# Splitting a fused retention and MLP kernel into up and down phases, with paired attention blocks, quadrant matmuls, DMA transposes and a half-chunk lead-in

## Chip, cores, metric

One core of one Trainium2 chip. The metric is the device time of one execution in microseconds. The profile gives a span, from the first to the last instruction, which is some 2 us shorter. In the profiles PE is the tensor engine (matmuls), DVE the vector engine, ACT the scalar engine, POOL or gpsimd the general one, and SP the one that only issues transfers. In the kernel before, all loads go out on gpsimd's DMA queue and the stores on SP's; the change puts the DMA transposes, and v of units 0 to 3, on SP's too.

## Reference

```python
# q, k, v: (8, 8, 576, 64); w_in: (512, 2048); w_out: (2048, 512)
scores = (q @ k.T) / 8
gamma  = 1 - 2.0 ** (-5 - arange(8))                 # one decay per head
ret    = scores * where(rel >= 0, gamma ** rel, 0)   # rel = query position - key position
x      = (ret @ v) as (4608, 512)                    # tokens x (heads * 64)
h      = x @ w_in
out    = (h * sigmoid(1.702 * h)) @ w_out            # float32
```

The attention is linear, so it runs in units of 128 tokens: scores inside a unit, plus an inter term, q times a running state of k and v from the units before. There are 36 units. Four units make a chunk of 512 tokens, and there are 9 chunks. The product with w_in is called the up projection, that with w_out the down projection, and `h * sigmoid(1.702 * h)` the Gelu; one "up" is the four matmuls that make 128 columns of `h` for a chunk.

## The kernel before

Each iteration `t` of one loop does one unit of attention on PE, a quarter of the up projection of one chunk and a quarter of the down projection of another, alternating.

```python
def transposes(u):                        # k and q: 8 transposes of 128x128 on PE
    for t, (src, nm) in enumerate(((kn[sl], "kn"), (qn[sl], "qn"))):
        for hp in range(HP):
            op("pe", lambda e, ...: e.matmul(psT[:, (1 - t) * HP + hp, :],
                src[:, 2 * hp : 2 * hp + 2, :], ident.ap(), is_transpose=True), ...)
    op("dve", lambda e: e.tensor_copy(qkT[u % 3].ap(), psT.ap()), ...)

def inter(u):                             # 4 matmuls of 128x128, zeros off the block diagonal
    ...
def scores(u):   ...                      # 8 matmuls, 64 rows each
def values(u):   ...                      # 8 matmuls, 64 columns each

load_qk(0); setup(); load_v(0)            # all loads on the gpsimd queue, in this order
for u in range(1, 4): load(u)
for i in range(4):
    load_win(i)
    load(4 + i)
for t in range(-2, NU + LAG):             # NU = 36, LAG = 12
    if t + 2 < NU: scale_v(t + 2)
    if 0 <= t < NU: state(t)
    if t + 2 < NU: transposes(t + 2)
    if 0 <= t < NU:
        state_out(t); inter(t)
        if t < 4: load_wout(t)
        load(t + NLD)                     # NLD = 8 load buffers
    ...                                   # scores of t + 1, values of t
    for s in range(4):
        if 0 <= ch < NCH: up(ch, 4 * hq + s, nh); ...
        if 0 <= co < NCH: down(co, r, s, bank)
    if 0 <= co < NCH: down_out(co, r, bank)
```

## Time and profile before

| | us |
|---|---|
| Median time (3 runs) | 338.76 |
| Span in the profile | 336.7 |
| First up matmul | 33.8 |
| 1152 projection matmuls of 512 columns, 0.863 us per four | 248.6 |
| One unit of attention on PE | 1.66 |

The page of the kernel before, in part: the busy tenths in 40 slices of 8.4 us, and who holds the chain that ended last.

```profile
PE   1676999999999999999999999999999999999995
DMA  9999999996666907667666907001000001011122
GB/s 83 190 196 218 215 210 214 221 202 88 98 88 86 153 31 98 91 95 93 95 93 94 158 31 95 31 33 31 33 31 33 31 34 62 31 33 62 62 94 64
...
PE 89%; POOL 6%; DMA 3%; ACT 0%; issue 0%; POOLq 0%
```

PE is full from the fifth slice on, and the chain is 89% PE: what comes off PE's stream comes off the time. For the first 75 us the loads keep the DMA engines over 90% busy, at about 210 GB/s.

The timeline of PE for one unit of attention before the change (start, duration, line, output and inputs). Matmuls are pipelined, so read the starts, not the durations.

```profile
141.54 0.39 PE L305 MATMUL psK<-vp,kn 128*128 128x128 bf16 x4
141.76 0.39 PE L293 MATMUL psT<-ident,kn 128*128 128x128 bf16 x4
141.98 0.39 PE L293 MATMUL psT<-ident,qn 128*128 128x128 bf16 x4
142.21 0.39 PE L326 MATMUL psO<-qkT,kv_1 128*128 128x128 bf16 x4
142.53 0.40 PE L342 MATMUL psS<-qkT 64*128 64x128 bf16 x8
142.85 0.24 PE L359 MATMUL psO<-pm_0,vp 128*64 128x128 bf16 x1
...
143.20 1.04 PE L374 MATMUL psH<-xT,w_in_sb 128*128 128x512 bf16 x4
```

The unit takes 143.20 - 141.54 = 1.66 us, of which the transposes are 0.44. Inter starts at 142.21 and four matmuls need 0.22, but scores start 0.32 later: 0.10 us is lost where the array shape changes from 128*128 to 64*128. The same happens at the next two changes of shape.

### The profile page before, as it was taken

The page shows a single profiled execution, that of the slowest core. Times are in us where ns is not written, and L with a number is a line of the kernel's source. Part 1 is how long each engine was busy: PE and PEld are TensorE (multiplying, and loading weights), DVE is VectorE, ACT ScalarE, POOL GpSimd, SP SyncE. Part 2 cuts the span into 40 slices and gives each one's busy share as a digit, 9 for nine tenths or more (in the row PEclk, how much of TensorE's full clock was granted, in tenths as well). Part 3 has the DMA queues.
Part 4 walks back from the last instruction along what each step waited for, and adds up shares of the span by engine and source line. Part 5 has one row for each costly group of instructions (what it writes and reads, how often), then busy time and mean ns, then how long its engine had stood idle before and what let it go on. Part 6 is the DMA issues. An engine that isn't in the chain of part 4 may idle for free.

```text
span 336.7 us, 5221 instructions
## 1 busy us (share of the span) xinstructions
PE 316.9 (94%) x2272; PEld 162.5 (48%) x2272; DVE 132.6 (39%) x229; ACT 115.4 (34%) x198; POOL 108.5 (32%) x135
## 2 busy tenths in 40 slices
PE   1676999999999999999999999999999999999995
PEld 0444455555555555555555555555555544443442
DVE  2687766864444434444444434444443200000000
ACT  5400345443333333333333333333333344442211
POOL 8999976842322514222322604000000000000000
PEclk9999999999999999999999999999999999999999
DMA  9999999996666907667666907001000001011122
GB/s 83 190 196 218 215 210 214 221 202 88 98 88 86 153 31 98 91 95 93 95 93 94 158 31 95 31 33 31 33 31 33 31 34 62 31 33 62 62 94 64
DMA packets 87447, 32.85 MB, mean 98 GB/s; under 512 B 76416, under 2 KB 80512, under 8 KB 87424
## 3 DMA queue, kind: packets, MB, share of 16 engines
q0 software_dynamic: 82176, 23.08, 60.3%
q1 hardware_dynamic: 5248, 9.44, 8.1%
q8 instruction: 18, 0.29, 0.4%
q14 instruction: 5, 0.04, 0.0%
HBM read 36.70 MB, written 9.44 MB: 137 GB/s over the span
## 4 chain that ended last, share of the span: by engine, by line
PE 89%; POOL 6%; DMA 3%; ACT 0%; issue 0%; POOLq 0%
PE psH L374 38%; PE psY L392 31%; PE psS L392 4%; PE psT L293 4%; PE psO L359 3%; DMA qn<-in_q_dram 3%; PE psS L342 3%; PE psO L392 2%; POOL kn L200 2%; PE psK L305 2%; POOL vn L214 2%; POOL qn L200 2%; PE psO L326 1%; POOL w_in_sb L223 1%; ACT osb L401 0%; PE psO L332 0%
## 5 line engine op out<-in xcount | busy, mean ns | idle before, releaser
L379 ACT ACTIVATE gT<-psH 128x512 bf16<-128x512 f32 x144 | 86.0, 597 | 182.9 <-PE psH L374 182.9
L374 PE MATMUL psH<-xT,w_in_sb 128*128 128x512 bf16 x576 | 145.1, 381 | 0.0
L392 PE MATMUL psY<-w_out_sb,gT 128*128 128x512 bf16 x480 | 122.2, 379 | 0.7 <-ACT osb L401 0.7
L374 PEld LDWEIGHTS psH<-xT,w_in_sb 128*128 128x128 bf16 x576 | 52.6, 98 | 65.4 <-ACT gT L379 5.1
L392 PEld LDWEIGHTS psY<-w_out_sb,gT 128*128 128x128 bf16 x480 | 46.5, 98 | 57.9 <-ACT osb L401 2.4
L296 DVE COPY qkT<-psT 128x1024 bf16<-128x1024 bf16 x36 | 24.8, 690 | 108.0 <-PE psT L293 107.9
L200 POOL DMA_DIRECT2D kn<-in_k_dram x40 | 36.8, 928 | 94.8 <-PE psK L305 80.3
L214 POOL DMA_DIRECT2D vn<-in_v_dram x40 | 37.4, 947 | 2.5 <-issue 2.4
L200 POOL DMA_DIRECT2D qn<-in_q_dram x40 | 37.0, 935 | 0.0
L284 DVE TENSOR_TENSOR vp<-vn,vfac 128x512 bf16<-128x512 f32 x36 | 24.6, 685 | 13.9 <-DMA vn<-in_v_dram 13.9
L368 DVE TENSOR_TENSOR xT<-psO,gq 128x512 bf16<-128x512 f32 x36 | 24.5, 680 | 6.0 <-PE psO L359 6.0
L293 PE MATMUL psT<-ident,kn 128*128 128x128 bf16 x144 | 15.5, 236 | 11.3 <-DVE ident L247 5.2
L401 ACT ACTIVATE osb<-psY 128x512 f32<-128x512 f32 x30 | 17.9, 597 | 14.0 <-PE psY L392 14.0
L350 DVE TENSOR_TENSOR pm_1<-psS,mask 128x512 bf16<-128x512 f32 x32 | 21.8, 680 | 0.0
L350 DVE TENSOR_TENSOR pm_0<-psS,mask 128x512 bf16<-128x512 f32 x32 | 21.8, 680 | 0.0
L293 PE MATMUL psT<-ident,qn 128*128 128x128 bf16 x144 | 15.5, 236 | 1.5 <-DMA qn<-in_q_dram 1.5
L293 PEld LDWEIGHTS psT<-ident,kn 128*128 128x128 bf16 x144 | 10.4, 105 | 13.3 <-DMA kn<-in_k_dram 8.6
L359 PE MATMUL psO<-pm_1,vp 128*64 128x128 bf16 x144 | 15.9, 237 | 0.0
L359 PE MATMUL psO<-pm_0,vp 128*64 128x128 bf16 x144 | 15.9, 237 | 0.0
L342 PE MATMUL psS<-qkT 64*128 64x128 bf16 x288 | 15.6, 233 | 0.0
L305 PE MATMUL psK<-vp,kn 128*128 128x128 bf16 x128 | 13.5, 233 | 2.0 <-DVE kv_0 L315 1.4
L305 PEld LDWEIGHTS psK<-vp,kn 128*128 128x128 bf16 x128 | 10.0, 103 | 9.6 <-DVE kv_0 L315 1.9
(44 smaller groups left out, 140.3 us busy)
## 6 DMA issues: line engine op xcount, KB each, us to landing
vn<-in_v_dram POOLq DMA_DIRECT2D x32, 256.0 KB, 5.0
out_dram<-osb SPq DMA_DIRECT2D x32, 256.0 KB, 2.0
kn<-in_k_dram POOLq DMA_DIRECT2D x32, 128.0 KB, 4.5
qn<-in_q_dram POOLq DMA_DIRECT2D x32, 128.0 KB, 5.2
w_in_sb<-in_moe_w_in_dram POOLq DMA_DIRECT2D x4, 512.0 KB, 10.1
w_out_sb<-in_moe_w_out_dram POOLq DMA_DIRECT2D x4, 512.0 KB, 15.5
vn<-in_v_dram POOLq DMA_DIRECT2D x8, 128.0 KB, 6.3
out_dram<-osb SPq DMA_DIRECT2D x8, 128.0 KB, 2.4
```

Of the source, the lines that this page charges most:

```text
L200: e.dma_start(dst[p0 : p0 + n, :, :], src[b, :, s0 : s0 + n, :].rearrange("h p d -> p h d"),)
L214: e.dma_start(vn[sl][p0 : p0 + n, :, :], v[b, :, s0 : s0 + n, :].rearrange("h p d -> p h d"),)
L284: op("dve", lambda e: e.tensor_tensor(vp[u % 3].ap(), vn[sl].ap(), vfac[:, ty, :, None].to_broadcast([P, H, DH]), ALU.mult), reads=[f"vn{s ...
L293: op("pe", lambda e, src=src, hp=hp, t=t: e.matmul(psT[:, (1 - t) * HP + hp, :], src[:, 2 * hp : 2 * hp + 2, :], ident.ap(), is_transpose= ...
L296: op("dve", lambda e: e.tensor_copy(qkT[u % 3].ap(), psT.ap()), reads=["psT"], writes=[f"qkT{u % 3}"])
L305: op("pe", lambda e, hp=hp: e.matmul(psK[:, hp, :], kn[sl][:, 2 * hp : 2 * hp + 2, :], vp[u % 3][:, 2 * hp : 2 * hp + 2, :], start=(c == 0 ...
L342: op("pe", lambda e, hp=hp, hh=hh: e.matmul(psS[hh][:, hp, :], qt[64 * hh : 64 * hh + 64, HP + hp, :], qt[64 * hh : 64 * hh + 64, hp, :], ...
L350: op("dve", lambda e, hh=hh: e.tensor_tensor(pm[u % 2][hh].ap(), psS[hh].ap(), m[:, None, :].to_broadcast([P, HP, P]), ALU.mult), reads=[f ...
L359: op("pe", lambda e, hp=hp, hh=hh: e.matmul(psO[64 * hh : 64 * hh + 64, hp, :], vp[u % 3][:, 2 * hp + hh, :], pm[u % 2][hh][:, hp, :], sta ...
L374: op("pe", lambda e, a=a: e.matmul(psH[n % 2].ap(), w_in_sb[:, a, P * f : P * f + P], xT[c % 3][:, a, :], start=(a == 0), stop=(a == HP - 1)),
L379: op("act", lambda e: e.activation(gT[c % 4][:, f, :], psH[n % 2].ap(), AF.Gelu_apprx_sigmoid), reads=[f"psH{n % 2}"], writes=[f"gT{c % 4} ...
L392: op("pe", lambda e, f=f: e.matmul(y, gT[c % 4][:, f, P * r : P * r + P], w_out_sb[:, f, :], start=(f == 0), stop=(f == NF - 1)), reads=[f ...
```

## The change

The intent: take the k and q transposes off PE (DMA transposes from unit 8 on), change the array shape less often (two units per attention block, placed in the down phase), shrink the inter term to eight 64x64 matmuls without the zeros, four at a time in the quadrants of the array, and start the first up phase on half a chunk. The diff is cut to its core. Left out are eight warm-up matmuls on PE at the start, the new table set-up, and the last chunk, whose final unit is done in two halves:

```diff
-    NLD = 8
+    NLD, NVP, NQT, NKV = 12, 8, 8, 8
+    NPE = 8
+        def dma_transpose(u):
+            op("sp", lambda e: e.dma_start_transpose(
+                kqT[u % NQT].ap(), kqn[sl].ap().rearrange("p t h d -> p (t h d)")), ...)
         def inter(u, slot):
-                        psO[:, hp, :], kv[kind][(c - 1) % 2][:, hp, :], qt[:, hp, :],
+                    for pb in range(2):
+                        for hh in range(2):      # 64x64 quadrants, banks X and Y by hh
+                                xbank(hh, slot)[64 * pb : 64 * pb + 64, g, t0 : t0 + n],
+                                kv[uv % NKV][64 * hh : 64 * hh + 64, hp, :],
+                                qt[64 * hh : 64 * hh + 64, HP + hp, t0 : t0 + n],
+        def block(j):                            # two units at once
+            inter(2 * j, 0); inter(2 * j + 1, 1)
+            for u, b in nxt: scores(u, b)        # of the next two units
+            values(2 * j, 0); values(2 * j + 1, 1)
+            ...
+        def lead_in():
+            load_kq(0, 0); load_kq(0, 1); load_v(0)      # load_v is on SP here
+            iota_small()
+            load_v(1, after=["kq0_1"])
+            load(1); iota_large(); load_win(0)
+            load_v(2, after=["kq1_1"]); load(2)
+            load_v(3, after=["kq2_1"]); load(3)
+            for i in range(1, 4): load_win(i)
+            for i in range(4): load_wout(i)
+            for u in range(4, NLD): load(u)
+            ...                                          # units 0 and 1
+            for f in range(4): up(0, f, 0, 2)            # half the chunk
+            for u in (2, 3):
+                transposes(u, "E", "B"); scale_v(u); score1(u); block1(u); state(u, "act")
+            for f in range(4, 8): up(0, f, 0, 2)
+            for f in range(8): up(0, f, 2, 4)
+            for f in range(8, NF): up(0, f)
+            for u in range(4): load(u + NLD)
+            work = {...}                                 # units 4 to 7, in pieces
+            for r in range(4):
+                for s in range(4): down(0, r, s, "AB"[r % 2]); ...
+                finish_unit(0, r, "AB"[r % 2])           # copy, then a store on SP
+        def steady():
+            for c in range(1, NCH):
+                for u in range(4 * c + 6 if c > 1 else NPE, min(4 * c + 10, NU)):
+                    dma_transpose(u)                     # on SP
+                for f in range(NF):
+                    up(c, f); ...                        # states, loads, v scaling
+                    if c == 1 and f == 8:
+                        scores(8, "CD"); scores(9, "EX"); ...
+                for r in range(4):
+                    for s in range(4):
+                        down(c, r, s, "AB"[r % 2])
+                        if s == 0 and r % 2 == 0: block(2 * c + 2 + r // 2)
+                    finish_unit(c, r, "AB"[r % 2])
```

## Prediction

> **What bounds it now.** The tensor engine: the chain of waits that ended last is 89% PE, and PE's timeline shows no gap from 33.8 us, the first up matmul, to almost the end of the 336.7 us span. The span (timeline, groups):
> - Lead-in, 33.8 us: PE waits for the loads of units 0 to 4 and for vector-engine copies. Gpsimd is busy throughout; each load costs it about 0.87 us to issue.
> - Projections: 1152 matmuls of 512 columns, 0.863 us per four: 248.6 us. The change leaves this work alone.
> - Attention on PE after the lead-in: 31 to 32 units of 1.66 us (141.54 to 143.20 us is one), about 51 us.
> - Tail: about 4 us after the last matmul starts.
>
> **One unit's 1.66 us.** State 0.22, transposes 0.44, inter 0.22, scores 0.22, values 0.25, and about 0.1 us empty at each of three changes of array shape. The Trainium skill, TensorEngine Tiling (Array Packing), section "Key Properties", says changing tiling mode drains the array; these gaps agree.
>
> **What changes on PE from unit 8 on (28 units).**
> - DMA transposes take 0.44 us per unit off PE: -12 us. They also remove a vector copy of 0.69 us per unit, off the path and worth nothing.
> - Inter in 64x64 quadrants: 0.22 falls to 0.11 to 0.2 if the quadrants overlap: -1 to -3 us.
> - Two units per block: four shape changes per pair instead of six: -3 us.
> - State moves into the up phase at the same cost.
>
> A two-unit block should take 1.5 to 1.7 us, so each of these units costs about 1.0 us instead of 1.66: about -18 us.
>
> Units 4 to 7 keep PE transposes and single-unit pieces inside the first down phase, about 1.75 us each: no gain. Separating up and down gains nothing itself: in the present up-only stretch (34 to 75 us) four ups take 3.46 us, full rate although weight loads wait up to 0.3 us for the Gelu (0.6 us each). Two banks just suffice.
>
> **Lead-in.** V loads 0 to 3 leave the gpsimd queue, and half a chunk can start after units 0 and 1. From the landings I estimate k and q of unit 1 at 8.5 us and the first up near 15 us, not 33.8. Units 2 and 3 then run as serial chains (transpose, ACT copy, scores, mask, values), about 4 us each, partly at half clock, with half-width ups limited by Gelu latency. Weights finish near 31 us. I expect the first down matmul near 41 us; less the 13.8 us of up work done by then, 27 us of lead-in remain: -7 us, four units' attention included.
>
> **Sum.** 27 + 248.6 + 7 (units 4 to 7) + 28 x 1.03 = 29 + 3.5 tail = 315 us, timed about 316.
>
> **Prediction: 316 us, 8 in 10 between 305 and 328. Faster by over 2%: 0.93; within 2%: 0.05; slower by over 2%: 0.02.**
>
> **What would show each step.** PE transposes only 64; blocks of 1.5 to 1.7 us in the down phases; inter matmuls starting four at a time; no PE gaps after about 42 us; first up near 15 us.
>
> **What would make it wrong.** Nothing in this trace times a DMA transpose. The Trainium skill, DMA: Bandwidth & Descriptors, section "DMA Transpose (X-bar)", only ties them to the hardware-generated queues. The first is issued after the first down phase's stores and needed about 7 us later, while loads still fill the queues; PE would stall near 65 us. Slow ones would also hold stores on SP, then output buffers. Other risks: quadrants that don't overlap (+3 us), Gelu too slow over 16 straight ups (+4), a lead-in longer or shorter by 5.

## Result and profile after

| | before | after |
|---|---|---|
| Median time, us | 338.98 (4 runs) | 334.75 (4 runs) |
| Span, us | 336.7 | 333.5 |
| First up / first down matmul, us | 33.8 / 76 | 18.4 / 48.0 |
| PE share of the chain | 89% | 83% |

The ratio is 0.987, with a 95% interval of 0.984 to 0.990. Ratios are the mean time of one kernel's fast runs over that of the other's of the same rounds, so not quite the ratio of the medians quoted. The result is correct, and the time lies outside the predicted range (305 to 328 us).

The same lines of the page after; its slices are 8.3 us.

```profile
PE   6365999984499999999999999999999999999996
DMA  9999999999999199339915992870170162011012
GB/s 99 158 194 202 209 213 224 234 231 135 100 131 202 64 175 177 100 97 166 180 65 130 188 156 65 132 88 34 66 158 2 63 80 47 2 63 63 2 31 94
...
PE 83%; DMA 9%; ACT 3%; DVE 2%; issue 2%; SPq 1%; POOL 0%; POOLq 0%
```

PE is weak in slices 1 to 4, as before, and has a new hole in slices 10 and 11, about 75 to 92 us. The third row falls to about half there, although the DMA row stays at 9.

The timeline of PE after, for a two-unit block in steady state. It lies between a down matmul group and the next one.

```profile
129.23 1.03 PE L468 MATMUL psA<-w_out_sb,gT 128*128 128x512 bf16 x4
130.18 0.24 PE L392 MATMUL psX<-kqT,kv 64*64 64x128 bf16 x1
130.19 0.24 PE L392 MATMUL psY<-kqT,kv 64*64 64x128 bf16 x1
130.19 0.24 PE L392 MATMUL psX<-kqT,kv 64*64 64x128 bf16 x1
130.19 0.24 PE L392 MATMUL psY<-kqT,kv 64*64 64x128 bf16 x1
130.26 0.22 PE L392 MATMUL psX<-kqT,kv 64*64 64x128 bf16 x1
...
130.42 0.23 PE L404 MATMUL psB<-kqT 64*128 64x128 bf16 x1
...
130.97 0.30 PE L423 MATMUL psX<-pm,vp 128*64 128x128 bf16 x4
...
131.54 0.60 PE L468 MATMUL psA<-w_out_sb,gT 128*128 128x512 bf16 x2
```

Four quadrant matmuls start within 0.01 us: they overlap. Four down matmuls need 0.86 us, so the block costs 131.54 - 129.23 - 0.86 = 1.45 us for two units; in this block only one unit has an inter term. This part of the change does what it was meant to do. From the first up matmul of chunk 2 (114.52 us) to that of chunk 3 (146.07 us) are 31.55 us. Less 27.62 for the projections, that leaves 0.98 us per unit, against 1.66 before.

Now the hole. The timeline of PE after, at its two gaps; the bracket gives the idle time before an instruction and what ended it.

```profile
77.19 0.81 PE L457 MATMUL psA<-xT,w_in_sb 128*128 128x512 bf16 x3
81.88 0.28 PE L404 MATMUL psC<-kqT 64*128 64x128 bf16 x1 [3.88 <-DMA kqT<-kqn]
...
87.89 0.28 PE L404 MATMUL psE<-kqT 64*128 64x128 bf16 x1 [5.40 <-DMA kqT<-kqn]
...
90.11 1.91 PE L457 MATMUL psA<-xT,w_in_sb 128*128 128x512 bf16 x4
```

The scores of units 8 and 9 wait for their DMA transposes. After that four up matmuls take 1.91 us instead of 1.03: the idle stretch has cost the full clock. The Trainium skill, TensorE: Matmul & The Clock Gate, section "Part 1: The HAM clock gate (the "warmup" mystery)", says that an idle array falls to half clock and needs a few microseconds of work to recover. The trace agrees: its clock record is at 0.5 from 80.4 us, 2.4 us into the first gap, to 94.0 us, 6.1 us after the second.

The chain of waits after, around the hole (start, duration, what):

```profile
69.20 0.82 PE psB L468 x3
70.02 0.02 issue
70.04 0.61 ACT osb L478
70.65 0.02 issue
70.67 0.33 SPq L484
...
71.11 1.54 SPq L342
...
72.76 15.07 DMA kqT<-kqn
87.84 0.05 issue
87.89 0.28 PE psE L404
```

Read downwards: the last down matmuls of the first down phase, their copy by ACT, their store issued by SP (L484). Only then do the transposes (L342) follow in SP's stream, the first at 71.11 us. The second one takes 15.07 us to land.

The up phase of chunk 1 lasted 27.82 us (69.84 to 97.66). The same phase without a stall takes 15.14 us, in the run hold_loads below. The hole therefore cost 12.7 us: 9.28 idle, the rest at half clock.

### The profile page after: what moved, and what is told of

Same layout as the page of the kernel before. It is cut to its first block, busy times and chain, and to the rows that moved or that the text cites. A ratio compares the mean times of both kernels' runs of the same rounds, so it can differ in the third digit from the quotient of the medians.

```text
span 333.5 us, 5231 instructions
## 1 busy us (share of the span) xinstructions
PE 301.1 (90%) x2198; PEld 144.8 (43%) x2232; DVE 119.3 (36%) x224; ACT 127.9 (38%) x230; POOL 107.3 (32%) x136
## 4 chain that ended last, share of the span: by engine, by line
PE 83%; DMA 9%; ACT 3%; DVE 2%; issue 2%; SPq 1%; POOL 0%; POOLq 0%
PE psA L468 19%; PE psB L457 18%; PE psA L457 18%; PE psB L468 18%; DMA kqT<-kqn 5%; DMA vn<-in_v_dram 3%; PE psK L353 2%; PE psX L423 2%; DVE pm L412 1%; PE psY L423 1%; PE psX L392 1%; PE psB L404 1%; DMA kqn<-in_q_dram 1%; PE psD L404 1%; ACT kqT L325 1%
## 5 line engine op out<-in xcount | busy, mean ns | idle before, releaser
L457 PE MATMUL psA<-xT,w_in_sb 128*128 128x512 bf16 (+1 forms) x297 | 76.8, 379 | 3.2 <-ACT gT L462 2.8
L457 PE MATMUL psB<-xT,w_in_sb 128*128 128x512 bf16 (+1 forms) x296 | 76.0, 379 | 0.7 <-issue 0.3
L468 PE MATMUL psA<-w_out_sb,gT 128*128 128x512 bf16 (+1 forms) x288 | 66.7, 373 | 2.2 <-issue 2.1
L209 POOL DMA_DIRECT2D kqn<-in_k_dram x40 | 35.5, 899 | 101.5 <-PE psK L353 91.6
L468 PE MATMUL psB<-w_out_sb,gT 128*128 128x512 bf16 (+1 forms) x285 | 63.9, 373 | 0.3 <-issue 0.2
L462 ACT ACTIVATE gT<-psB 128x512 bf16<-128x512 f32 (+1 forms) x76 | 43.7, 574 | 37.4 <-PE psB L457 37.1
L462 ACT ACTIVATE gT<-psA 128x512 bf16<-128x512 f32 (+1 forms) x76 | 43.7, 574 | 21.8 <-PE psA L457 21.7
L468 PEld LDWEIGHTS psA<-w_out_sb,gT 128*128 128x128 bf16 x304 | 28.2, 98 | 31.4 <-ACT gT L462 1.0
L468 PEld LDWEIGHTS psB<-w_out_sb,gT 128*128 128x128 bf16 x288 | 27.9, 98 | 31.5
L478 ACT ACTIVATE osb<-psA 128x512 f32<-128x512 f32 x18 | 10.7, 597 | 71.3 <-PE psA L468 71.3
L209 POOL DMA_DIRECT2D kqn<-in_q_dram x40 | 35.3, 889 | 2.6 <-issue 2.6
L412 DVE TENSOR_TENSOR pm<-psC,mask 128x512 bf16<-128x512 f32 x20 | 13.7, 683 | 22.0 <-PE psD L404 22.0
```

Of the source, the lines that this page charges most:

```text
L209: e.dma_start(kqn[sl][p0 : p0 + n, which, :, :], src[b, :, s0 : s0 + n, :].rearrange("h p d -> p h d"),)
L412: op("dve", lambda e: e.tensor_tensor(pm[u % 4][hh].ap(), ps32(banks[hh]).rearrange("p (a i) -> p a i", i=P), m[:, None, :].to_broadcast([ ...
L457: op("pe", lambda e, a=a: e.matmul(bank[b][:, n0:n1], w_in_sb[:, a, P * f : P * f + P], xT[c % 2][:, a, n0:n1], start=(a == 0), stop=(a == ...
L462: op("act", lambda e: e.activation(gT[c % 2][:, f, n0:n1], bank[b][:, n0:n1], AF.Gelu_apprx_sigmoid), reads=[b], writes=[f"g{c % 2}_{f}_{j ...
L468: op("pe", lambda e, f=f: e.matmul(bank[b][:, 0 : n1 - n0], gT[c % 2][:, f, P * r : P * r + P], w_out_sb[:, f, n0:n1], start=(f == 0), sto ...
L478: op("act", lambda e: e.activation(dst, src, AF.Copy), reads=[b], writes=[f"osb{i}_{n0}"])
```

## Experiments

"First down" is the start of the first down matmul, the end of the lead-in.

| run | median, us | span, us | ratio to before (95%) | first down, us |
|---|---|---|---|---|
| the change | 334.75 | 333.5 | 0.987 (0.984 to 0.990) | 47.96 |
| early_T | 324.85 | 323.7 | 0.958 (0.955 to 0.961) | 48.31 |
| hold_loads | 323.30 | 321.1 | 0.955 (0.951 to 0.958) | 47.66 |
| pe10 | 324.44 | 322.8 | 0.957 (0.954 to 0.961) | 48.97 |
| all_pe | 339.03 | 337.5 | 1.000 (0.998 to 1.003) | 49.08 |
| v1_early | 320.84 | 320.3 | 0.946 (0.943 to 0.948) | 45.86 |
| v_all_early | 322.27 | 320.7 | 0.950 (0.947 to 0.953) | 47.31 |
| v_pool | 318.78 | 317.5 | 0.940 (0.935 to 0.945) | 43.68 |
| lead_act | 318.84 | 318.4 | 0.940 (0.937 to 0.943) | 44.37 |
| lead_pipe | 315.79 | 314.1 | 0.930 (0.928 to 0.932) | 41.17 |
| best | 313.07 | 311.5 | 0.923 (0.917 to 0.929) | 36.74 |
| before_dmaT | 344.37 | 343.0 | 1.014 (1.008 to 1.020) | |

All outputs are right. Landing times below come from the completion records of each load's semaphore in the trace, counted from the start of the span.

### The hole: late issue, full queues, or slow transposes?

**early_T**, on the change:

```diff
+            dma_transpose(8)
+            dma_transpose(9)
             work = {
 ...
                 finish_unit(0, r, "AB"[r % 2])
+                if r < 2:
+                    dma_transpose(10 + r)
```

> The transposes of units 8 and 9 are issued on SP before the first store of the first down phase, and 10 and 11 between its stores, instead of all after its last store (71.1 us). Theory A (late issue: the transpose of unit 8 has only 7 us until its scores need it, and takes 10.7): no PE gap above 1 us between 70 and 100 us, no half-clock stretch after it, span 333.5 - 12.4 = 321 us. Theory B (capacity: loads and transposes starve each other in whatever order, so the stall only moves): part of the stall comes back, span 327 or more.

The span was 323.7 us and the hole is gone: the up phase of chunk 1 takes 15.15 us. But two smaller waits for transposes appear later, 1.50 us at 118.5 and 0.62 us at 128.7, and they account for most of the missing 3 us. Theory A carries most of it, theory B some: a part of the stall moved. Unit 8 still needed 9.5 us (issued at 51.5, landed at 61.0); it only had the time.

**hold_loads**, on the change: the transposes are issued where they were, and the loads of units 12 to 18 wait for the transpose of unit 9.

```diff
-            for u in range(4):
-                load(u + NLD)
-                (2, 2): lambda: (block1(5), score1(6), state(5), load(16), load(17)),
+                (2, 2): lambda: (block1(5), score1(6), state(5)),
 ...
                 for u in range(4 * c + 6 if c > 1 else NPE, min(4 * c + 10, NU)):
+                    if u == 10 and c == 1:
+                        held.append("T1_0")      # load 12 reads it: it waits for unit 9's transpose
+                        load(12)
+                        held.clear()
+                        for n in range(13, 19): load(n)
                     dma_transpose(u)
```

(The load of unit 18 left `work` in the same way.)

> The transposes are issued as late as in the changed kernel, but the loads of units 12 to 18 are held until the transpose of unit 9 has landed, so the DMA queues are nearly empty when it is issued. If the long landing (10.7 us) comes from sharing the DMA engines with the loads, unit 8 lands about 3 us after issue (the least seen in this trace), the PE gap near 78 us falls below 1 us, span about 321 to 323. If the landing time belongs to the transpose itself or to SP, it still lands near 82 us and the span stays near 333.

The span was 321.1 us. The timeline of PE in hold_loads at the place of the hole:

```profile
76.68 1.03 PE L459 MATMUL psA<-xT,w_in_sb 128*128 128x512 bf16 x4
77.64 0.23 PE L406 MATMUL psC<-kqT 64*128 64x128 bf16 x1
```

No wait is left here (one of 0.36 us for a transpose comes at 117.9). Issued at 70.83 us, unit 8 landed at 74.22, 3.4 us later, against 10.7 in the change. So the issue was as late as before, and that alone did no harm; the loads in the same queues did. In views by stretch of 10 us (PE, PEld, DVE, ACT, POOL busy; PE clock; DMA share; GB/s), first the change:

```profile
60.00:70.00 10.00, 8.83 (x103) 4.74 (x104) 8.40 (x19) 2.76 (x5) 10.00 (x14) 1.00 1.88 242
80.00:90.00 10.00, 2.39 (x19) 1.27 (x21) 2.58 (x4) 0.00 (x0) 2.65 (x3) 0.52 1.69 110
```

then hold_loads:

```profile
60.00:70.00 10.00, 8.83 (x104) 4.68 (x105) 8.43 (x18) 2.71 (x6) 0.00 (x0) 1.00 0.09 32
70.00:80.00 10.00, 9.84 (x64) 4.27 (x64) 4.10 (x9) 6.32 (x11) 3.97 (x5) 1.00 1.07 149
90.00:100.00 10.00, 9.84 (x88) 4.92 (x87) 4.47 (x8) 1.61 (x3) 10.00 (x13) 1.00 1.87 231
```

A share above 1 means that packets overlap on an engine. In the change, loads and output stores without transposes (60 to 70) move 242 GB/s at a share of 1.88; by the packet records 187 of it are loads and 52 stores. Loads and transposes together (80 to 90) move 110 GB/s at nearly the same share. They slow each other down: the loads of units 18 and 19, issued at 67.7 to 75.0 us, took 21 to 25 us to land, those issued at 55.8 to 62.7 took 13. In hold_loads the queues are almost idle at 60 to 70 (32 GB/s), the transposes pass quickly, and the held loads then run (231 GB/s with the stores) and still arrive in time. The slowness is not only of the first transposes: later in hold_loads, beside loads again, those issued at 102.8 to 112.5 us take 9.7 to 14.5 us to land. They are issued long enough before they are needed.

**pe10**, on the change: units 8 and 9 on PE, DMA transposes from unit 10.

```diff
-    NPE = 8
+    NPE = 10
+                    if c == 1 and f in (1, 5):
+                        transposes(8 + f // 4, "E", "E", "dve", "dve")
```

> Units 8 and 9 are transposed on PE (8 more matmuls each, 0.9 us in all); DMA transposes start with unit 10, issued at the same late place. Theory A: units 10 and 11 are needed only in the first block of the next down phase, some 15 us after issue: no stall above 1 us, span about 322. Theory B: they land late too (10 to 16 us each, one after the other), and a stall of several us shows before the first block; span 326 or more.

The span was 322.8 us, with no wait for a transpose. Unit 10 still took 9.5 us to land (issued at 72.1, landed at 81.6), but it was needed only at 87. The up phase of chunk 1 takes 16.03 us, 0.89 more than in hold_loads: the added PE work.

**all_pe**, on the change: no DMA transposes at all.

```diff
-                for u in range(4 * c + 6 if c > 1 else NPE, min(4 * c + 10, NU)):
-                    dma_transpose(u)
+                    if f % 4 == 1:
+                        for u in ((4 * c + 6 + f // 4,) if c > 1 else (
+                                (8, 9), (10,), (11, 12), (13,))[f // 4]):
+                            if u < NU: transposes(u, "E", "E", "dve", "dve")
```

> No DMA transposes at all: units 8 to 35 are transposed on PE in the up phases, copied by DVE. If the accounting is right, 28 x 0.44 = 12.3 us of PE work come back and the 12.4 us of stall and half clock go: span 333.5 within 2 us, no PE gap above 1 us after 48 us. If the transposes on PE are hidden somewhere, the span falls to about 321.

The span was 337.5 us, 4.0 us above the change and outside the expected band. A chunk takes 33.34 us (108.65 to 141.99) instead of 31.55, which is 0.45 us more per unit: the saving by DMA transposes is real, and close to the 0.44 of the prediction. The rest of the miss is new: 2.5 us of PE gaps in the up phase of chunk 1, where two units share the accumulator bank E for their transposes, and the lead-in ended 1.1 us later. In the change, then, the DMA transposes roughly paid for the hole they made (28 x 0.45 = 12.6 us against 12.7), and no more.

**before_dmaT**, on the kernel before: only the DMA transposes.

```diff
-            if t + 2 < NU:
+            if t + 2 < min(8, NU):
                 transposes(t + 2)
+            if 8 <= t + 4 < NU:
+                dma_transpose(t + 4)     # k and q, on SP; qkT has 6 buffers instead of 3
```

> The kernel before, with only the DMA transposes from unit 8 added (k and q of a unit as two transposes, issued on SP four units ahead). If a DMA transpose saves the 0.44 us of PE per unit wherever the rest is the same, 28 x 0.44 = 12.3 us: 338.8 - 12.3 = 326.5 us. If transposes and loads starve each other in the first 80 us also here, PE gaps show before 100 us and less is gained.

It gained nothing: 344.37 us against 338.65, 1.4% slower (0.8 to 2.0), which the 2% rule calls unclear. The timeline of PE in before_dmaT, the three large gaps and one unit later on:

```profile
53.80 0.61 PE L349 MATMUL psS<-qkT 64*128 64x128 bf16 x8 [5.81 <-DMA qkT<-qn]
...
64.60 0.40 PE L349 MATMUL psS<-qkT 64*128 64x128 bf16 x8 [3.98 <-DMA qkT<-qn]
...
79.37 0.61 PE L349 MATMUL psS<-qkT 64*128 64x128 bf16 x8 [3.88 <-DMA qkT<-qn]
...
98.09 0.40 PE L349 MATMUL psS<-qkT 64*128 64x128 bf16 x8
...
106.22 0.40 PE L349 MATMUL psS<-qkT 64*128 64x128 bf16 x8
```

13.7 us are lost while the loads fill the queues, plus half clock around each gap (51.9 to 58.7, 65.5 to 68.9 and 79.2 to 82.6 us in the clock record; it begins 3.7 to 4.9 us after PE went idle, the second time only when PE was back at work). Later one iteration, a unit with its ups and downs, takes 8.13 us (98.09 to 106.22) against 8.58 in the kernel before (141.54 to 150.12). So both halves of the account show here without any other part of the change: 0.45 us per unit gained, and more than that lost in the stretch where loads and transposes meet.

### The lead-in

These runs start from hold_loads, so that the hole does not hide them. In the change, v of unit 1 was issued at about 6.3 us, after q of unit 0, and landed only at 15.65 us. PE waited 4.6 us for the masked scores of unit 1, which DVE computes after it has scaled that v.

**v1_early**: `load_v(1, after=["kq0_1"])` becomes `load_v(1)`.

> On top of hold_loads (321.1 us, first down matmul at 47.7 us): the v load of unit 1 is issued at once on SP instead of after q of unit 0 has landed. Theory C (the 4.5 us wait before the values of unit 1 is this late load, and the lead-in is one chain): values of unit 1 near 13.5 us instead of 16.6, first down matmul 3 to 4 us earlier. Theory D (the chain is bound again later by the v load of unit 3, which is gated the same way and landed at 30.2 us): that gap closes but the first down matmul comes only about 1 us earlier, near 46.5 us, span about 320.

Theory D held. V of unit 1 landed at 5.3 us and the gap closed, but the first down matmul moved only from 47.66 to 45.86 us: a new wait of 1.68 us, behind v of unit 3 (landed at 28.0), took over.

**v_all_early**: the same for units 2 and 3.

> On top of hold_loads: the v loads of units 1, 2 and 3 are all issued at once on SP. Theory D: v of unit 3 lands by about 12 us, nothing waits for it, and the first down matmul comes 3 to 4 us earlier than in hold_loads, near 44 us, span about 317.5. If instead these loads only push k and q of units 1 to 3 back by the same time (the DMA engines are the limit), the first down matmul stays near 47.

No gain. V of unit 3 landed at 9.9 us, but k and q of unit 0 landed at 7.2 and 9.2 us, against 5.8 and 6.7 in v1_early. The work was pushed back at the start of the chain instead.

**v_pool**: v of units 1 to 3 on the gpsimd queue.

```diff
-            load_v(1, after=["kq0_1"])
             load(1)
+            load_v(1, eng="pool")
 ...
-            load_v(2, after=["kq1_1"])
             load(2)
+            load_v(2, eng="pool")        # and 3 in the same way
```

> On top of hold_loads: v of units 1 to 3 is loaded through the gpsimd queue, right after k and q of its unit, as in the kernel before, instead of on SP behind a wait. In these traces a v load through gpsimd moves 4096-byte packets, on SP 256-byte packets that share the engines [...]with the weights. If that sharing is what made v of unit 1 (9.4 us) and of unit 3 (9.6 us) slow, v of unit 1 lands near 10 us and of unit 3 near 19 us at 0.9 us more issue time each, and the first down matmul comes 3 to 4 us earlier, near 44 us, span about 317.5. If the DMA engines are simply full then, v of unit 1 lands near 15 us again and nothing is gained.

As expected: v of unit 1 landed at 9.6 us, 4.3 us after its issue at 5.3, and of unit 3 at 20.9 us, 8.5 us after its issue at 12.4. The first down matmul came at 43.68 us. In hold_loads the two took 9.2 us (6.0 to 15.25) and 11.5 us (18.4 to 29.8; the 9.6 of the expectation is too low). So v of unit 1 gained mostly by landing faster, but v of unit 3 mostly by being issued 6.0 us earlier, without its gate. The DMA records show 4096-byte packets for these loads and 256-byte packets for v loaded on SP. The Trainium skill, DMA: Bandwidth & Descriptors, section "Queues, rings and completion order", says each engine takes turns between queues packet by packet. If a packet of the records is one of these packets, then by estimate the 256 KB of one v need 64 turns on each of the 16 engines in small packets, and 4 in large ones. The records show the two queues interleaved, but not one for one: between 9.3 and 11.3 us 287 packets of v against 222 of the weights (1024 bytes each) in hold_loads, 601 against 167 in the change. The run also changed the gating of the loads together with their queue, so that packet size is the cause is not shown.

**lead_act**, on v_all_early: DVE copies unit 1's transposes; the last tables and the Gelu table are loaded while ACT waits.

```diff
-            transposes(1, "E", "B")
+            transposes(1, "E", "B", "dve", "dve")
             block1(0)
             state(0, "act")
+            for a in range(4): gq_tail(a)
+            op("act", lambda e: e.activation(gT[1][:, 0, 0:1], lnsc.ap(), AF.Gelu_apprx_sigmoid), ...)
```

> On top of v_all_early: DVE instead of ACT copies the transposes of unit 1, and the last gq tables and the Gelu table load are done while ACT waits for unit 1. The 2.5 us that PE waits for the first Gelu should go, and unit 1's scores come about 1 us earlier; the first down matmul is 2 to 4 us earlier than in v_all_early, near 41 us, then bound by the landing of q of unit 2 (18.6 us) and the two serial chains.

(The old place of the `gq_tail` loop, after unit 1, is removed; the cut doesn't show it.) The 2.5 us wait for the first Gelu is down to 0.37, and the first down matmul moved from 47.31 to 44.37 us. That is the gain expected (2 to 4 us) but not the place (41).

**lead_pipe**, on lead_act:

```diff
-            for u in (2, 3):
-                transposes(u, "E", "B"); scale_v(u); score1(u); block1(u); state(u, "act")
-            for f in range(4, 8): up(0, f, 0, 2)
-            for f in range(8): up(0, f, 2, 4)
-            for f in range(8, NF): up(0, f)
+            transposes(2, "E", "B", "act", "dve"); scale_v(2); score1(2)
+            transposes(3, "E", "A", "act", "dve"); scale_v(3)
+            block1(2); state(2, "act"); score1(3); block1(3); state(3, "act")
+            for f in range(4): up(0, f, 2, 4)
+            for f in range(4, NF): up(0, f)
```

> On top of lead_act: units 2 and 3 overlap (transposes of 3 before the values of 2, k copied by ACT and q by DVE), and f 4 to 7 of the first up phase run at full width. The chain of two units shortens by about 3 us and the half-width ups by about 1 us: first down matmul near 37 to 38 us, span about 311 to 312, unless the down phase then waits for w_out (39.7 us) or for k of unit 4 (40.6 us).

The first down matmul came at 41.17 us, 3.2 us earlier than in lead_act, which is the first half of the expectation (3 + 1); the absolute figure started again from a base 3 us too optimistic.

**best**, on lead_pipe: v of unit 1 on SP at once, v of units 2 and 3 on gpsimd.

> lead_pipe, with v of unit 1 alone issued at once on SP (it landed at 5.3 us in v1_early and cost k of unit 0 1 us instead of 2.3) and v of units 2 and 3 on the gpsimd queue behind their k and q. The first chain starts about 2 us earlier than in lead_pipe: first down matmul near 39 us instead of 41.2, span near 312, if the landing of q of unit 2 does not bind.

Better than expected: first down matmul at 36.74 us, span 311.5 us. The first up matmul is 2.9 us earlier than in lead_pipe. The rest goes with the clock: the third half-width up takes 0.61 us in the timeline, against 1.04 in lead_pipe, and the work after it runs at full clock, in lead_pipe only from about 26.2 us. No run isolates this. This is the fastest version, 7.7% below the kernel before. The rest of a stall is still in it, 1.36 us at 83.9 us.

## Why the prediction was wrong

The prediction's sum against the trace of the change, in us:

| term | predicted | measured | how |
|---|---|---|---|
| lead-in, less up work | 27 | 34.2 | 47.96 - 13.81 |
| projections | 248.6 | 248.6 | 1152 x 0.2158 |
| units 4 to 7 | 7 | 8.1 | first down phase, 21.88 - 13.81 |
| stall for DMA transposes | 0 | 12.7 | up phase of chunk 1, 27.82 against 15.14 in hold_loads |
| units 8 to 35 | 29 | 27.3 | the rest; 28 x 0.98 gives 27.4 |
| tail | 3.5 | 2.7 | 333.5 - 330.84, the end of the last matmul |
| sum | 315 | 333.5 | |

- **Right: what bounds the kernel, and what a unit costs.** PE bounds it, a unit's share fell from 1.66 to 0.98 us, the quadrants overlap, and 16 straight ups run at full rate. all_pe and before_dmaT confirm 0.45 us per unit for the transposes.
- **Failed step: the cost of the DMA transposes, taken as zero in the sum.** The prediction named the danger ("PE would stall near 65 us") and the 7 us between issue and need, but put it under the risks and counted the whole -12 us as gain, although the trace of before showed the queues full until about 75 us. The runs put 12.7 us in its place. early_T, hold_loads and pe10 each remove 10 to 12 us of it, by issuing earlier, by emptying the queues, and by not needing the first two. hold_loads shows that the landing time depends on the loads in flight: 3.4 us against 10.7 at the same late issue. The lateness only makes it visible.
- **Mis-sized term: the lead-in, 27 against 34.2.** The prediction counted only that the v loads leave the gpsimd queue. In fact v of unit 1 landed at 15.65 us and of unit 3 at 30.2, both gated and slow. The serial chains also ran largely at half clock (0.5 in the clock record from 8.7 to 25.7 and from 29.2 to 36.0 us, in spite of the warm-up matmuls, after which it shows full clock from 5.3 to 8.7), and PE waited 2.5 us for the first Gelu behind a table load. With the lead-in pipelined, lead_pipe gives 314.1 us, close to the predicted sum, but only because it repairs both terms.

Open: how the DMA engines share between loads and transposes (only the totals are shown), whether packet size or gating made the v loads slow, and how much of the lead-in is half clock alone. The clock record has no entry for the first part of several runs: the kernel before shows 9 tenths there, while four 128-column matmuls take 0.61 us instead of 0.39.

## What to carry to other kernels

Work that is taken off the bounding engine and given to the DMA queues is not free while loads use these queues: look at the queues' share in the stretch where the first such transfer is issued, and ask when it is needed. Give the first transfers an empty queue by holding back loads that are not yet needed, and put them ahead of stores that wait for computation in the issuing engine's stream. A gap of a few microseconds on PE (3.9 to 5.8 us here) costs more than itself, because matmuls after it run at half clock. In a lead-in, check which load the last link waits for before moving any other; closing one gap may only uncover the next.

## What the Trainium skill lacked or had wrong

- Advanced Engine Details and Errata, section "X-Bar Transpose (TRN2)", says transpose DMAs are as fast as regular ones. The runs do not test that in quiet queues: in hold_loads two 256 KB transposes landed 1.4 us apart (74.22 and 75.63 us), but SP also issued them 1.5 us apart. It does not hold beside the loads of this kernel: 10.7 us from issue to landing against 3.4 without them, and 110 GB/s in total against 242 for loads and stores without transposes.
- DMA: Bandwidth & Descriptors, section "Rules for kernel authors", says a transpose next to ordinary DMAs needs nothing. All runs here were correct, so the rule holds for the data; that row has no word on time. In before_dmaT the neighbourhood cost 13.7 us of waits.
- The same page has no figure for a load of short runs on the SP queue beside a busy gpsimd queue: 256 KB in 256-byte packets took 9.2 and 11.5 us here (v of units 1 and 3 in hold_loads), and 4.3 and 8.5 us through the gpsimd queue in 4096-byte packets (v_pool, issued 0.7 and 6.0 us earlier and ungated).
- TensorEngine Tiling (Array Packing), section "Key Properties", says that a change of tiling mode drains the array, without a figure: about 0.10 us per change in these traces.
